# Windowed attention and a spatial-gating MLP on one core: batch 0's v in two long-run loads turned on chip, batch 0 in token halves, and a new order of the head

## Chip, cores and metric

One Trainium2 chip, one core. The metric is device microseconds from start to end of one execution, as the median of the runs shown. The engines are PE (matrix multiply), DVE (vector), ACT (scalar, activation functions), POOL (GpSimd) and SP (SyncE), on whose queue nearly all transfers are issued. Times called profile are from one profiled execution.

## What is computed

Eight batches of 8 heads, sequence 576, head width 64: causal attention over a window of 64 tokens, then a gated MLP whose gate mixes tokens.

```
scores = scale * np.matmul(q, k.transpose(0, 1, 3, 2))
mask = (rel >= 0) & (rel < window)              # rel = query - key, window = 64
attn = softmax(where(mask, scores, -1e9))
x = matmul(attn, v), heads side by side          # (8, 576, 512)
h = np.maximum(x @ w_in, 0.0)                    # (8, 576, 1024)
u, v = h[..., :512], h[..., 512:]
v_n = (v - mean(v)) / sqrt(var(v) + 1e-6)        # over the 512 features
v_s = np.einsum('ts,bsd->btd', w_spatial, v_n) + b_spatial[None, :, None]
out = (u * v_s) @ w_out                          # (8, 576, 512)
```

## The kernel before

The whole program is a list of steps, and its order is written out by hand. The string ORDER (from line 18) holds words such as `V0_2:PE:1`: step, engine, buffer or PSUM bank. Each engine executes its own steps in the order in which they stand there; between engines a step waits for the steps that it depends on and for its buffers. `PE` and `PH` are both the matmul engine (PH: a matmul of 128 output rows written as two of 64 that run side by side). `DQ` words are transfers on SP's queue, in the order written. There a transfer also waits until the one issued eight places before it has landed. PSUM is four single banks and two pairs.

The names, with batch b, head group g (four heads) and head pair u:

- **Loads.** `ldq`, `ldk` (L412) bring 128 x 1152 f32, 576 KB, in long runs: partition (head, 32 groups of 18 tokens). `ldv` (L433) brings v in token order instead, five transfers for each group: four of 128 tokens x 4 heads x 64 (128 KB, in runs of 256 bytes) and a last one of 64 tokens. `st` are the output stores (L656, L662).
- **Attention.** `cq`, `ck` cast q and k to f16 (ACT L292, DVE L300, POOL L295 in three parts); `tq`, `tk` are DVE's 32 x 32 stream transpose (L419). `cv` casts v to hv; `sl`, `su`, `s4` copy hv shifted by 64 partitions into hs. `S` scores (PE L479), `S_r` those of the last 64 tokens (L553); `E` exp (ACT L486, er L563); `M` the mask, a minimum (DVE L489, er L574); `Z` column sums (PE L502, L582), `N` and `n` their inverse by a logarithm and an exponential on ACT (L529, L531); `P` e times v (PE L514, edge P_r L597); `X` P times the inverse, x in f16 (DVE L522, edge X_r L606).
- **gMLP.** `V` and `U` are x times the two halves of w_in, by 128 tokens j or 128 features i (helper lines 614 and 617; the last 64 tokens of V at L702, fused with the batch before's O at L705). `Vr`, `Ur` are the relus on ACT (L669, L763), `Vb`, `Va` statistics (DVE L671, L673), `L1`, `L2` the inverse deviation (ACT L716, L718), `A` the normalisation to vn (DVE L728). `G` multiplies by the transposed w_spatial, `Ge` by u (DVE L797), `O` by w_out, `Oe` copies the result out of PSUM (ACT L647). `W`, `We` transpose w_spatial (PE L378) and copy it out; `cwin`, `cwsp`, `cwo` cast weights.
- **Fillers.** `D` are matmuls of a zero scratch tile (L862): 27 steps of two 512-column matmuls, two of them (D25, D26) of nine 128-column ones. Most stand in the head, D9 ahead of the first V, D17 ahead of G0.

Batch b+1's attention is threaded through batch b's gMLP. `V0_j` waits for all four `X0` (both head pairs of both groups), `U0_i` likewise, `O0_j` for all four `G0` tiles. `P3_r`, the edge P of batch 3, needs hs of v3, and so the copies `cv3_00` (POOL) and `su3_00` (ACT) behind the loads of v3.

Of the kernel before, what the change touches and what calls it, by code (L numbers as in the profile page):

```python
# [26 lines left out]
N0_01:ACT:2 cv0_00:ACT:1 N0_11:ACT:3 ldwin101:DQ su0_11:DVE M0_10:DVE D12:PE:0 Z0_10:PE:2 D20:PE:1
sl0_11:POOL tk1_0:DVE:4 sl0_00:ACT:1 N0_10:ACT:4 n0_11:ACT n0_10:ACT cq1_0:POOL:2 tq1_0:DVE:5
ldq1_1:DQ:2 ldk1_1:DQ:3 P0_10:PE:0 P0_11:PE:3 cwin110:ACT n0_01:ACT D11:PE:1 cv0_01:POOL
ldwin000:DQ:4 ldwin010:DQ:5 ldwin001:DQ ldwin011:DQ ldwsp1:DQ:6 X0_10:DVE:0 su0_00:DVE X0_11:DVE  # L30
n0_00:ACT sl0_01:POOL cb:POOL su0_01:POOL S1_0:PE:0:1 D25:PE:2 D13:PE:1 P0_00:PE:0 X0_00:DVE:1
E1_01:ACT:3 s40_1:ACT P0_01:PE:2 D9:PE:3 cwin111:POOL cwin100:POOL cwin101:POOL ck1_1:POOL:1
s40_0:ACT E1_00:ACT:2 cwin010:POOL X0_01:DVE cwin001:POOL cwin011:POOL V0_2:PE:1 M1_01:DVE
Vr0_2:ACT:0 n0_r:ACT P0_r:PE:3 Z1_01:PE:0 V0_0:PE:2 ldwsp3:DQ:0 M1_00:DVE N1_01:ACT:5 Vr0_0:ACT:1
cq1_1:DVE:3 Z1_00:PE:1 V0_3:PH:0 V0_1:PE:2 N1_00:ACT:4 cwin000:ACT Vr0_3:ACT:2 Vr0_1:ACT:3
ldwsp0:DQ:7 ldwsp4:DQ:1 ldwsp2:DQ:2 cwsp1:POOL:6 ldv1_00:DQ:2 ldq2_0:DQ:3 X0_r:DVE:0 tq1_1:DVE:7
Vb0_2:DVE:0 V0_4:PE:3 tk1_1:DVE:8 S1_1:PE:1:0 cwsp3:POOL:0 cwsp0:POOL:1 Vb0_0:DVE:1 Vb0_3:DVE:2
Vr0_4:ACT:4 Va0_3:DVE Vb0_4:DVE:3 Va0_4:DVE Va0_0:DVE Va0_2:DVE Vb0_1:DVE:4 Va0_1:DVE U0_2:PH:1
U0_3:PH:0 ldk2_0:DQ:4 U0_4:PE:2 ldv1_01:DQ ldv1_02:DQ ldv1_03:DQ E1_11:ACT:1 E1_10:ACT:0 cwsp2:POOL
cq2_0:POOL:0 M1_10:DVE ldv1_10:DQ:3 Ur0_2:ACT:0 L10:ACT:0 ldv1_11:DQ ldv1_12:DQ ldv1_13:DQ L20:ACT  # L40
ldv1_14:DQ ldq2_1:DQ:5 ldv1_04:DQ ldk2_1:DQ:6 ldwo00:DQ:0 ldwo01:DQ Ur0_4:ACT:1 S1_r:PE:0:1
Z1_10:PE:3 U0_0:PE:1 ldwo10:DQ:7 ldwo11:DQ U0_1:PE:2 E1_r0:ACT:0 Ur0_3:ACT:2 E1_r1:ACT Ur0_0:ACT:3
N1_10:ACT:3 A0_0:DVE:0 A0_3:DVE:1 cwsp4:DVE Ur0_1:ACT:4 W1:PE:0 W3:PE:1 W2:PE:3 W0:PE:2 A0_1:DVE:2
A0_4:DVE M1_11:DVE We1:DVE M1_r:DVE n1_00:ACT We2:ACT We3:ACT A0_2:DVE:3 We0:DVE W4:PE:0 ldq3_0:DQ:1
ldk3_0:DQ:2 ldv2_00:DQ:1 ck2_0:POOL:2 We4:DVE D17:PE:3 Z1_11:PE:1 Z1_r:PE:2 G0_0:PH:3 G0_1:PH:0
tq2_0:DVE:2 n1_10:ACT N1_11:ACT:0 tk2_0:DVE:3 Ge0_0:DVE:0 cv1_00:ACT:2 n1_01:ACT sl1_00:POOL:2
n1_11:ACT su1_00:ACT N1_r:ACT:2 cv1_01:POOL Ge0_1:DVE:1 su1_01:DVE G0_3:PH:1 sl1_01:POOL
cv1_10:ACT:3 Ge0_3:DVE:2 cv1_11:DVE S2_0:PE:0:1 P1_01:PE:2 P1_00:PE:3 X1_00:DVE:2 G0_2:PH:0
sl1_10:POOL:3 ldv2_01:DQ ldv2_02:DQ su1_10:ACT sl1_11:ACT E2_01:ACT:3 n1_r:ACT su1_11:POOL
s41_1:POOL P1_10:PE:1 X1_01:DVE P1_11:PE:3 G0_4:PE:2 X1_10:DVE:3 X1_11:DVE U1_1:PH:1 cq2_1:POOL:3  # L50
# [150 lines left out]
def kernel(  # L201
# [419 lines left out]
    def xr(b, r):  # L621
        return XB[b, r // 2].t[:, r % 2, :]
# [295 lines left out]
```

## Time and profile before

| what | us |
|---|---|
| median of three runs | 195.78 |
| the three runs | 195.34, 195.78, 196.4 |
| span of the profiled execution | 193.6 |
| the median less that span | 2.18 |
| PE busy, DVE busy, ACT busy, POOL busy | 184.9, 163.7, 157.1, 87.4 |

The span is the stretch that the profiler shows from first to last instruction; the execution's own time, measured outside, holds some 2 us more. A row of a timeline gives the start, the busy time, the engine, the line, the operation with its tiles and count, and in brackets how long the engine was idle before it and what released it. Matmul ends are modelled, so starts are the better measure on PE: the length of a row includes some time under the next one.

### The profile page before, as it was taken

The numbers are of one execution on the slowest core, as the hardware profiler recorded it, in microseconds if no ns is written. First come the engines' busy times: TensorE is split into PE (matmuls) and PEld (weight loads), VectorE is DVE, ScalarE is ACT, GpSimd is POOL, SyncE is SP. The second block draws the span as 40 slices with busy tenths as digits, with TensorE's granted clock in tenths as the row PEclk, the third lists the DMA queues.
The fourth block names the chain that finished last, engine by engine and source line by source line (L and its number), as shares of the span: only waits on it lengthen the run. The fifth ranks groups of instructions, "written<-read, shape, count | busy, mean of one in ns | idle before, by whom it ended". The sixth has DMA issues, their size and how long they took to land.

```text
span 193.6 us, 7606 instructions
## 1 busy us (share of the span) xinstructions
PE 184.9 (95%) x3218; PEld 107.0 (55%) x3218; DVE 163.7 (85%) x304; ACT 157.1 (81%) x282; POOL 87.4 (45%) x161
## 2 busy tenths in 40 slices
PE   7798998999999999999999999999999999999991
PEld 2352534556556664656665656565756565665560
DVE  4899899999999999998999999998996967468331
ACT  2269998998999999899979999999999875706430
POOL 4027775849932986701956577615641520000000
PEclk9999999999999999999999999999999999999999
DMA  5999999899989997619987999669958000600445
GB/s 177 373 316 290 391 355 333 168 275 373 242 205 332 261 335 179 149 38 289 367 230 184 310 310 282 196 177 218 306 125 266 22 3 0 224 30 0 135 166 191
DMA packets 50421, 42.73 MB, mean 221 GB/s; under 512 B 39377, under 2 KB 39761, under 8 KB 50386
## 3 DMA queue, kind: packets, MB, share of 16 engines
q1 hardware_dynamic: 50162, 42.04, 73.3%
q8 instruction: 25, 0.41, 0.9%
q10 hardware_dynamic: 224, 0.20, 0.3%
q14 instruction: 10, 0.08, 0.1%
HBM read 32.79 MB, written 9.44 MB: 218 GB/s over the span
## 4 chain that ended last, share of the span: by engine, by line
PE 70%; DVE 13%; ACT 9%; DMA 3%; issue 2%; SPq 1%
PE bank L617 50%; PE bank L614 4%; PE pair L479 4%; PE bank L514 3%; DMA nk<-in_k_dram 3%; PE bank L502 3%; ACT e L486 3%; DVE qT L419 2%; PE bank L702 2%; DVE e L489 2%; DVE kT L419 2%; DVE st L671 2%; DVE g L797 1%; DVE x L522 1%; ACT lz L529 1%
## 5 line engine op out<-in xcount | busy, mean ns | idle before, releaser
L617 PE MATMUL bank<-wspT,vn 128*64 128x512 f16 (+3 forms) x530 | 39.1, 296 | 0.0
L486 ACT ACTIVATE e<-pair 128x1024 f16<-128x1024 f32 x32 | 32.0, 1030 | 1.6 <-PE pair L479 1.4
L797 DVE TENSOR_TENSOR g<-bank,ru 128x512 f16<-128x512 f32 (+1 forms) x36 | 23.3, 654 | 9.4 <-PE bank L617 7.0
L647 ACT COPY ob<-bank 128x512 f32<-128x512 f32 (+1 forms) x38 | 21.9, 591 | 9.7 <-PE bank L617 8.4
L669 ACT ACTIVATE vs<-bank 128x512 f16<-128x512 f32 (+1 forms) x40 | 23.8, 602 | 7.1 <-PE bank L705 5.6
L617 PE MATMUL bank<-x,win 128*64 128x512 f16 (+2 forms) x304 | 29.1, 327 | 0.0
L617 PEld LDWEIGHTS <-vn 128*64 128x64 f16 (+1 forms) x530 | 20.8, 111 | 13.2 <-issue 0.2
L671 DVE BATCH_NORM_STATS2 st<-vs 128x6 f32<-128x512 f16 (+1 forms) x40 | 26.0, 670 | 2.3 <-ACT vs L669 2.2
L298 POOL COPY hs<-hv 64x512 f16<-64x512 f16 (+1 forms) x36 | 20.1, 585 | 16.3 <-ACT hv L292 8.4
L617 PE MATMUL bank<-win,x 128*64 128x512 f16 x216 | 27.0, 379 | 0.0
L617 PE MATMUL bank<-wout,g 128*64 128x512 f16 (+1 forms) x208 | 24.7, 371 | 0.0
L522 DVE TENSOR_TENSOR x<-bank,lz 128x512 f16<-128x512 f32 x32 | 21.2, 684 | 3.5 <-PE bank L514 2.2
L489 DVE TENSOR_TENSOR e<-e,mask 128x1024 f16<-128x1024 f16 x32 | 23.0, 725 | 0.5 <-ACT e L486 0.4
L763 ACT ACTIVATE ru<-bank 128x512 f32<-128x512 f32 (+1 forms) x38 | 21.6, 584 | 1.5 <-PE bank L617 0.8
L295 POOL CAST hk<-nk 128x384 f16<-128x384 f32 x36 | 19.4, 574 | 7.1 <-DMA nk<-in_k_dram 6.7
L529 ACT ACTIVATE lz<-bank 128x512 f32<-128x512 f32 x32 | 19.0, 599 | 1.9 <-PE bank L502 1.6
L298 POOL CAST hv<-nv 128x512 f16<-128x512 f32 x18 | 11.7, 661 | 18.8 <-DMA nv<-in_v_dram 18.7
L419 DVE STREAM_TRANSPOSE kT<-hk 128x576 f32<-128x576 f32 x16 | 19.9, 1241 | 0.2 <-ACT hk L292 0.2
L419 DVE STREAM_TRANSPOSE qT<-hq 128x576 f32<-128x576 f32 x16 | 19.8, 1237 | 0.2
L531 ACT ACTIVATE lz<-lz 128x512 f32<-128x512 f32 x32 | 19.6, 642 | 0.0
L295 POOL CAST hq<-nq 128x384 f16<-128x384 f32 x27 | 14.9, 588 | 10.3 <-DMA nq<-in_q_dram 7.8
L617 PEld LDWEIGHTS <-win 128*64 128x64 f16 x304 | 14.4, 110 | 9.2
(91 smaller groups left out, 298.9 us busy)
## 6 DMA issues: line engine op xcount, KB each, us to landing
nk<-in_k_dram SPq DMA_DIRECT2D x16, 576.0 KB, 6.6
nq<-in_q_dram SPq DMA_DIRECT2D x16, 576.0 KB, 6.1
nv<-in_v_dram SPq DMA_DIRECT2D x64, 128.0 KB, 5.9
out_dram<-ob SPq DMA_DIRECT2D x14, 512.0 KB, 5.8
wi<-in_moe_w_in_dram SPq DMA_DIRECT2D x8, 256.0 KB, 5.8
ws<-in_moe_w_spatial_dram SPq DMA_DIRECT2D x4, 288.0 KB, 7.6
nv<-in_v_dram SPq DMA_DIRECT2D x16, 64.0 KB, 4.5
wo<-in_moe_w_out_dram SPq DMA_DIRECT2D x4, 256.0 KB, 7.2
```

Of the source, the lines that this page charges most:

```text
L295: nc.gpsimd.tensor_copy(o[:, n:n + 384], i[:, n:n + 384])
L298: nc.gpsimd.tensor_copy(o[:, lo:hi, :, :], i[:, lo:hi, :, :])
L419: d = add(f"t{name}{b}_{g}", ("DVE", 1.09), key, lambda e: nc.vector.transpose(qt.t[:, :].rearrange("p (i j) -> p j i", j=18), h.t[:, :].b ...
L486: ex = add(f"E{b}_{g}{u}", ("ACT", 0.91), key, lambda e, u=u: nc.scalar.activation(e2[u].t[:, :, :], sc[u].t[:, :, :], AF.Exp, bias=0.0, s ...
L489: mins.append(add(f"M{b}_{g}{u}", ("DVE", 0.65), key, lambda e, u=u: nc.vector.tensor_tensor(e2[u].t[:, :, :], e2[u].t[:, :, :], mask[:, : ...
L522: lambda e, u=u, ob=ob, lz=lz: nc.vector.tensor_tensor(x.t[:, u, :], ob.t[:, :], lz.t[:, :], ALU.mult),
L617: nc.tensor.matmul(o[c:c + 64, :], w[:, c:c + 64], x, start=start, stop=stop)
L647: lambda e: (nc.vector.tensor_copy if last else nc.scalar.copy)(view(), m.t[rows, 0:n]),
L669: rl = add(f"Vr{b}_{j}", ("ACT", 0.49), key, lambda e: nc.scalar.activation(vs.t[0:jn, :], m.t[0:jn, :], AF.Relu), deps=[pv], acq=[vs], us ...
L671: s1 = add(f"Vb{b}_{j}", ("DVE", 0.6), key + 0.02, lambda e: nc.vector.bn_stats(st6.t[0:jn, 0:6], vs.t[0:jn, :]), deps=[rl], acq=[st6], us ...
L763: lambda e, m=m, ru=ru, n=n: nc.scalar.activation(ru.t[:, 0:n], m.t[:, 0:n], AF.Relu), deps=[pu], acq=[ru], uses=[m])))
L797: nc.vector.tensor_tensor(g.t[:, 0:n], m.t[:, 0:n], ru.t[:, 0:n], ALU.mult)
```

## The change

Six things, all but the last for batch 0 alone.

1. Its v is loaded like q and k (`ldvt0_0`, `ldvt0_1`, 128 x 1152), cast to f16 (`cvt`: group 0 on ACT, group 1 on POOL), turned in 32 x 32 blocks on DVE (`tvt`), then in 128 x 128 blocks on PE (`T0_g` eight, `T0_g4` two), and copied out of PSUM into hv by `cv0_00`, `cv0_01` (ACT) and `cv0_10`, `cv0_11` (DVE), every second element; `s40_g` copies out of PSUM on ACT. Ten small loads and two POOL casts of v go.
2. `Z0`, `P0`, `X0` work on both head pairs of one 256-token half instead of one head pair over 512 tokens. `V0_j` and `U0_i` then need the X of one half only; `U0`, `G0` and `O0` go by 256 tokens, with twice as many matmuls of 256 columns in U and G.
3. The relus and `Oe` may be put on DVE by the order; it puts them on ACT as before.
4. Fillers: 23 steps, all of two 512-column matmuls, D0 to D22, none behind the first V.
5. Casts move: `ck0_0`, `cq0_1` to ACT, `ck1_0`, `cq1_1` to POOL, and `ck0_1` to POOL.
6. ORDER is written anew. On PE the first part differs; from about G1_1 and V2_3 on it is the same sequence of steps. On SP the order differs further on.

The core of the diff:

```diff
+SPLIT = (0,)
+TURN = (0,)
+        if b in TURN:
+            vt, vd = one("vt", v, key + 0.002)
...
+                    for w in (0, 1):
+                        nc.tensor.transpose(o[0:sn, at + 128 * w:at + 128 * w + 128],
+                                            vT[:, 128 * c:128 * c + sn, w], id16[:, :])
...
+                        lambda e, lo=lo, hi=hi: cp(
+                            e, hv.t[:, lo:hi, :, :].rearrange("p c h (x w) -> p c w (h x)", w=2),
+                            m.t.bitcast(f16)[:, 256 * lo:256 * hi].rearrange(
+                                "p (c w x) -> p c w x", w=2, x=128)),
...
+                    for hh in range(4):
+                        w, p = hh % 2, hh // 2
+                        nc.tensor.matmul(zb.t[64 * w:64 * w + 64, 256 * p:256 * p + 256], ones[:, :],
+                                         e2[p].t[:, w, 256 * u:256 * u + 256], start=True, stop=True)
...
-                     deps=[XD[b, r] for r in range(4)] + [WIN[1, r] for r in range(4)],
+                     deps=[XD[b, r] for r in (range(4) if b not in SPLIT else (j // 2, 2 + j // 2))]
+                     + [WIN[1, r] for r in range(4)],
...
+                    if i < 4 and b in SPLIT:
+                        u = i // 2
+                        for f in (0, 1):
+                            c = 2 * (i % 2) + f
+                            for r in range(4):
+                                halves(f"U{b}_{i}", m.t[:, 256 * f:256 * f + 256],
+                                       w_in_sb[r][:, 128 * c:128 * c + 128],
+                                       xr(b, r)[:, 256 * u:256 * u + 256], r == 0, r == 3)
...
-            for c in range(2 if i < NWARM - NFILL else FILL):
-                n = 512 if i < NWARM - NFILL else 128
-                nc.tensor.matmul(m.t[:, 0:n], scratch[:, 0:128], scratch[:, 0:n], start=True, stop=True)
+            for c in range(2):
+                nc.tensor.matmul(m.t[:, :], scratch[:, 0:128], scratch[:, :], start=True, stop=True)
```

DVE up to batch 0's X, before (e2_0 are the masked scores, kT and qT the transposes for batch 1, hs the shifted copies of v, x0_0 and x0_1 batch 0's x of groups 0 and 1):

```order
L300 CAST hk1_0_285<-nk1_0_156 128x1152
L574 TENSOR_TENSOR er_0_275<-er_0_275,mask_88 128x512
L489 TENSOR_TENSOR e2_0_11_359<-e2_0_11_359,mask_88 128x1024
L300 COPY hs0_1_279<-hv0_1_154 64x512
L489 TENSOR_TENSOR e2_0_10_365<-e2_0_10_365,mask_88 128x1024
L419 STREAM_TRANSPOSE kT1_0_400<-hk1_0_285 128x18x32
L419 STREAM_TRANSPOSE qT1_0_412<-hq1_0_408 128x18x32
L522 TENSOR_TENSOR x0_1_461<-bank0_69,lz0_10_404 128x512
L300 COPY hs0_0_402<-hv0_0_385 64x512
L522 TENSOR_TENSOR x0_1_461<-bank3_72,lz0_11_387 128x512
L522 TENSOR_TENSOR x0_0_552<-bank0_69,lz0_00_357 128x512
L522 TENSOR_TENSOR x0_0_552<-bank2_71,lz0_01_383 128x512
```

The same place in the changed kernel (x0_4 is the x of the last 64 tokens):

```order
L302 COPY hv0_1_421<-bank3_72 128x2x2x128 x2
L539 TENSOR_TENSOR e2_0_11_389<-e2_0_11_389,mask_88 128x1024
L539 TENSOR_TENSOR e2_0_10_419<-e2_0_10_419,mask_88 128x1024
L302 COPY hs0_1_441<-hv0_1_421 64x512
L430 STREAM_TRANSPOSE kT1_0_455<-hk1_0_315 128x18x32
L302 COPY hs0_1_441<-hv0_1_421 64x512
L430 STREAM_TRANSPOSE qT1_0_487<-hq1_0_402 128x18x32
L576 TENSOR_TENSOR x0_0_517<-bank2_71,lz0_00_386 128x2x256
L727 TENSOR_TENSOR x0_4_580<-bank0_69,lz0_r_443 128x256
L576 TENSOR_TENSOR x0_1_600<-bank1_70,lz0_10_460 128x2x256
L576 TENSOR_TENSOR x0_0_517<-bank3_72,lz0_01_457 128x2x256
L576 TENSOR_TENSOR x0_1_600<-bank2_71,lz0_11_489 128x2x256
```

The cast of k1_0 has left DVE, the two evictions of turned v (x2 in the first row) have come, and the x of the last 64 tokens stands second among the X, where before it stood behind batch 1's masks. The order by token halves lets the first two V steps do with the first three X rows.

SP's queue around the loads of v3, before (nv3_0 is v of batch 3, group 0; ob are output tiles):

```order
L662 DMA out_0_dram<-ob0_0_1547 128x2x512
L433 DMA nv3_0_1936<-in_v_dram 128x4x64
L433 DMA nv3_1_1466<-in_v_dram 64x4x64
L433 DMA nv3_0_1936<-in_v_dram 128x4x64 x3
L433 DMA nv4_0_2045<-in_v_dram 128x4x64 x2
L433 DMA nv3_0_1936<-in_v_dram 64x4x64
L656 DMA out_0_dram<-ob1_4_1977 64x512
```

And in the changed kernel:

```order
L783 DMA out_0_dram<-ob0_2_1443 128x2x512
L777 DMA out_0_dram<-ob1_4_2061 64x512
L488 DMA nv4_0_1395<-in_v_dram 128x4x64
L783 DMA out_0_dram<-ob0_0_1650 128x2x512
L488 DMA nv3_0_2112<-in_v_dram 128x4x64 x2
L488 DMA nv3_0_2112<-in_v_dram 64x4x64
L488 DMA nv3_0_2112<-in_v_dram 128x4x64
L488 DMA nv3_1_1299<-in_v_dram 64x4x64
L488 DMA nv3_0_2112<-in_v_dram 128x4x64
```

The store of batch 1's last 64 tokens (`st1_4`, ob1_4) stood behind the loads of v3 and now stands ahead of all six of them.

406 lines of the change are left out of this document (260 added, 146 removed).

## The prediction

> **What bounds the kernel now.** I read the page's busy shares first, then the busy time of each engine by stretch, then the timeline of the matmul engine (PE) around its gaps, and last the timelines of the engine or queue that each gap names.
>
> ```profile
> span 193.6 us, 7606 instructions
> PE 184.9 (95%) x3218; PEld 107.0 (55%) x3218; DVE 163.7 (85%) x304; ACT 157.1 (81%) x282; POOL 87.4 (45%) x161
> ```
>
> The shares say PE; where it has room only the stretches tell (columns: start:end, length, busy PE, PEld, DVE, ACT, POOL with counts, granted clock, DMA share, GB/s).
>
> ```profile
> 10.00:20.00 10.00, 9.25 (x145) 4.15 (x143) 9.80 (x14) 8.34 (x14) 5.38 (x8) 1.00 1.13 307
> ...
> 24.00:30.00 6.00, 5.56 (x47) 2.14 (x51) 5.57 (x8) 5.49 (x10) 4.56 (x7) 1.00 1.08 339
> ...
> 46.00:80.00 34.00, 33.95 (x584) 19.51 (x580) 33.03 (x60) 32.59 (x62) 23.35 (x42) 1.00 0.92 264
> 80.00:90.00 10.00, 9.67 (x250) 6.36 (x247) 9.48 (x18) 9.31 (x15) 2.10 (x4) 1.00 0.47 106
> 90.00:186.00 96.00, 96.00 (x1677) 57.66 (x1674) 79.41 (x152) 77.89 (x142) 35.58 (x67) 1.00 0.63 184
> ```
>
> From 46 to 186 us PE is idle for 0.05 + 0.33 us; so a microsecond won before 46 reaches the end unless something else holds PE later. In the head the busy PE is mostly filler (L862); what bounds there is DVE, 9.80 of 10 us. So three places matter: when the first real gMLP matmul starts, what PE loses or wastes between it and batch 1's first U, and the one later gap, near 86.6. PE's rows there (start, length, what ended the idle time):
>
> ```profile
> 9.26 0.67 PE L479 MATMUL pair<-qT,kT 32*128 32x128 f16 x56 [1.12 <-DVE qT L419]
> ...
> 23.42 0.39 PE L614 MATMUL bank<-win,x 128*128 128x512 f16 x1
> 24.02 0.82 PE L614 MATMUL bank<-win,x 128*128 128x512 f16 x3 [0.21 <-DVE x L522]
> 24.77 0.32 PE L597 MATMUL bank<-er,hs 128*64 128x64 f16 x8
> 24.92 0.39 PE L502 MATMUL bank<-e,ones 128*64 128x512 f16 x2
> ...
> 28.37 1.05 PE L702 MATMUL bank<-win,x 128*64 128x512 f16 x4
> 29.85 0.67 PE L479 MATMUL pair<-qT,kT 32*128 32x128 f16 x56 [0.42 <-DVE kT L419]
> ...
> 32.30 0.64 PE L614 MATMUL bank<-x,win 128*128 128x64 f16 x16
> ...
> 33.41 0.41 PE L502 MATMUL bank<-e,ones 128*64 128x512 f16 x2 [0.24 <-DVE e L489]
> ...
> 37.80 0.61 PE L862 MATMUL bank<-scratch 128*128 128x512 f16 x2
> 38.34 0.41 PE L502 MATMUL bank<-e,ones 128*64 128x512 f16 x2
> ...
> 45.53 1.05 PE L617 MATMUL bank<-x,win 128*64 128x512 f16 x8
> ```
>
> V of batch 0 starts at 23.42, halts for an X, waits 0.42 for batch 1's k transpose and 0.24 for a masked e; one filler (D17) stands in the stream at 37.80; batch 1's U starts at 45.53.
>
> **The change part by part.** *A, up to the first V.* Loads and the chain to the first S (SyncE's queue, DVE, ACT):
>
> ```profile
> 1.21 0.38 SPq L412 DMA_DIRECT2D nk<-in_k_dram  x1
> ...
> 2.10 0.43 SPq L412 DMA_DIRECT2D nk<-in_k_dram  x1
> ...
> 5.26 0.76 DVE L300 CAST hk<-nk 128x1152 f16<-128x1152 f32 x1 [1.66 <-DMA nk<-in_k_dram]
> 8.20 1.15 ACT L292 CAST hk<-nk 128x1152 f16<-128x1152 f32 x1 [6.11 <-DMA nk<-in_k_dram]
> 10.00 1.94 ACT L486 ACTIVATE e<-pair 128x1024 f16<-128x1024 f32 x2 [0.65 <-PE pair L479]
> 9.38 1.26 DVE L419 STREAM_TRANSPOSE kT<-hk 128x576 f32<-128x576 f32 x1 [0.18 <-ACT hk L292]
> ...
> 13.83 0.69 DVE L489 TENSOR_TENSOR e<-e,mask 128x1024 f16<-128x1024 f16 x1
> ...
> 22.67 1.29 DVE L522 TENSOR_TENSOR x<-bank,lz 128x512 f16<-128x512 f32 x2 [0.18 <-PE bank L514]
> ```
>
> The first k lands 4.05 us after its issue, and the second k, two big loads on, 2.94 later: 1.47 each. The changed queue starts with q, k, v, k, q, v, k, q; with the first issue 0.4 earlier they land at about 4.9, 6.3, 7.8, 9.3, 10.7, 12.2, 13.7 and 15.1. The second load is cast on ACT (1.15) to 7.5 and transposed (1.26) to 8.8, which starts the first S, against 9.26. E starts 0.74 after S (10.00 − 9.26) and takes about 1.0, so the first mask starts near 10.55. From there I take DVE as unbroken: four masks and the edge mask at 0.65, five transposes at 1.15 (back to back they come at less than the row's 1.26), four hs copies at up to 0.29, two evictions of turned v, then X0_00 0.65 and X0_r 0.4, behind which V0_4 can start; X0_10 is done inside V0_4's four matmuls.
>
> The evictions have no row in before. The nearest is DVE copying 128 x 576 f16 out of a bank with a plain destination (here with the hs copies, from the groups that keep shapes apart); the other bound is the 0.69 of the mask above:
>
> ```profile
> L300 DVE COPY hs<-hv 64x512 f16<-64x512 f16 x4 | 1.2, 294 | 0.1
> L300 DVE COPY wspT<-bank 128x576 f16<-128x576 f16 x2 | 0.9, 450 | 0.1
> ```
>
> That is 0.40 for 512 columns, to 0.69; the new copy writes every second element, so I take 0.55. [...]
>
> Sum: 3.25 + 5.75 + 1.1 + 1.1 + 1.05 = 12.25, so V0_4 at 22.8 if DVE never waits; it waited 0.18 + 0.31 + 0.18 in before's head, and I allow 0.2: 23.0. **A is −0.4** (−0.9 with quick evictions and short masks, +0.9 with slow Pool casts, below). Masks come one for one as before; DVE loses four casts (0.76 each) and gains two transposes and two evictions (3.4), so its work is about equal: the gain is order, and X0_01, which held the first V, is now behind it. The PE transposes of v (20 short matmuls) take the place of fillers. Splitting Z, P, U, G by 256 columns adds matmuls but no columns; the 16-matmul row at 32.30 shows 64-column matmuls each with its own weight load at 0.04 us, so loads do not limit 256-column ones: 0 us.
>
> *B, from the first V to U of batch 1.* Starts less work give the stalls: 23.42 to 24.02 is 0.60 for one matmul of some 0.22 (1.05 for four against 0.82 for three), 0.38 lost; the wait of S at 29.85 is 0.42, that at 33.41 is 0.24; D17 is 38.34 − 37.80 = 0.54; P0_r (24.77 to 24.92, 0.15) moves ahead of V. Sum 1.73. All go: V0_4 goes first, S1_1 stands behind more gMLP work, D17 is dropped. What is late next: G0 comes earlier and needs A, cast weights and their transposes, and S1_r and Z1_01 now stand among U: I charge 0.3 (0 to 0.7, an estimate from the stalls they replace, 0.24 and 0.42). **B is −1.45.** The new cover is thin: DVE was 5.57 of 6 busy there.
>
> *C, the gap near 86.6.* Batch 3's edge P stands behind hs of v3:
>
> ```profile
> 67.06 10.66 SPq L433 DMA_DIRECT2D nv<-in_v_dram  x8
> ...
> 74.88 0.58 ACT L647 COPY ob<-bank 64x512 f32<-64x512 f32 x1
> ...
> 78.57 0.61 POOL L298 CAST hv<-nv 128x512 f16<-128x512 f32 x1 [0.33 <-DMA nv<-in_v_dram]
> ...
> 85.43 1.04 ACT L292 COPY hs<-hv 64x1024 f16<-64x1024 f16 x1
> 86.62 0.32 PE L597 MATMUL bank<-er,hs 128*64 128x64 f16 x8 [0.33 <-DVE e L489]
> ```
>
> The page's list of transfers (count, KB, median us from issue to landing) has the two kinds that matter:
>
> ```profile
> nv<-in_v_dram SPq DMA_DIRECT2D x64, 128.0 KB, 5.9
> ...
> out_dram<-ob SPq DMA_DIRECT2D x8, 128.0 KB, 3.4
> ```
>
> In before the v3 loads went ahead of the store st1_4, whose data is ready at 75.46. In the changed queue this store stands ahead of them: all six v loads queue behind a wait on ACT, and the last, six rows later on a queue where each transfer also waits for the one eight rows back, follows close on the store's landing. With A and B won the store goes at 73.5 and lands 3.4 later; the last v load issues at about 77 and lands 3.4 to 5.9 later, 80.4 to 82.9; cast 0.61 and hs copy 1.04 give 82.1 to 84.6, against 86.47 − 1.9 = 84.6 needed. **C is 0, to +0.3.** Elsewhere the order of PE's work is the same from V2 on, and its 96.00 of 96 us carries the gain to the end; the tail has the same steps.
>
> Sum: −0.4 − 1.45 + 0 = −1.9 on the 193.6 us span, 191.7. The three runs' median is 195.78 (195.34 to 196.4), 2.2 more than the span; I take this as fixed: **193.9 us**.
>
> **The rivals.** *Pool casts set the head.* The change gives Pool the casts of k0_1, v0_1, k1_0 and q1_0 in a row, then three hs copies and four w_in casts that every V needs. Pool's three-part casts cost 1.41 in a quiet stretch, and far more where loads and DVE are busy:
>
> ```profile
> 21.69 1.72 POOL L300 CAST win<-wi 128x512 f16<-128x512 f32 x3
> 25.20 2.28 POOL L295 CAST hk<-nk 128x384 f16<-128x384 f32 x3 [1.79 <-DMA nk<-in_k_dram]
> ...
> 34.13 2.69 POOL L295 CAST hq<-nq 128x384 f16<-128x384 f32 x3 [1.39 <-DMA nq<-in_q_dram]
> ...
> 75.53 1.41 POOL L295 CAST hq<-nq 128x384 f16<-128x384 f32 x3
> ```
>
> The first starts when k0_1 lands, at 9.3, the second not before 12.2. At 1.41 the four end at 16.5; three hs copies (some 0.55 each, as the weight casts) and four weight casts, 2.3, bring it to 20.5; at 2.28 it is 19.1 and 23.1, just in time; at 2.69: 12.0, 14.9, 17.6, 20.3, then 4.0 of copies and weights, 24.3. V0_4 then starts 1.3 late, and −1.9 becomes −0.6: **195.2**. Against it: the head's casts would meet a Pool with half its time free (5.38 of 10). [...]
>
> *A larger gain.* Quick evictions, no waits of DVE, no new stalls in B: −0.9 − 1.7 = −2.6, **193.2**. For it: the stream after V is otherwise the same work. Against: DVE has no slack to hide anything.
>
> *The slow side: the store ahead of the v3 loads.* If they issue at the rate of the row at 67.06 (10.66 over 8, 1.33 each) from 74.5, the sixth goes at 82.5; landing 4.7 later (middle of 3.4 and 5.9), cast and copy bring hs to 88.8 against 86.47 in before. PE stands still at P3_r, all of A and B is lost and 2.3 more: **198.1**. It decides once v3's last load lands after 84.8. For it: DMA busy 0.92 from 46 to 80, and this gap already exists. Against: those 10.66 us held waits of the queue that need not recur, and from 80 DMA share is 0.47.
>
> *The change does nothing for the time*: the head wins, but DVE and ACT (33.03 and 32.59 of 34 us from 46 to 80) turn out to set batches 1 and 2, and both only move work about: **195.8**.
>
> **How the numbers follow.** A measurement of this kernel can tell about 0.5% from no change, 0.98 us: faster is below 194.8, slower above 196.8. Chances: forecast (193.3 to 194.8) 0.5; larger gain (below 193.3) 0.13; Pool casts or saturated DVE and ACT (194.8 to 196.8) 0.22; slow side 0.15. So faster 0.63, same 0.22, slower 0.15. The range runs from 192.7 (just past the larger gain, its lowest part, some 0.04, left out) to 196.9 (the slow side left out). The forecast's own range is 193.3 to 194.8.
>
> **What would show it.** Right: V0_4 near 23.0 with no hole behind it, batch 1's first U near 43.6, P3_r near 84.7, span near 191.7. Wrong in A: idle DVE ahead of a transpose, released by Pool; V0_4 waiting for a win cast on Pool. Wrong in B: new PE waits for A, Ge or hs of batch 1 between 25 and 45. Wrong in C: P3_r's idle time over 1 us, with v3 loads issued after 79. If U1 gains 2 us and P3_r starts where it did, C has eaten it.

## The result, and the profile after

The changed kernel is slower: a median of 203.22 us (200.95 to 203.97, four runs) against 196.09 (195.34 to 197.63) for the kernel before in the same comparison, a ratio of 1.031 [1.023, 1.039]. The forecast was 193.9 with 192.7 to 196.9 around it; even the rival on the slow side, at 198.1, was too low. The profiled execution is the longest of the four (203.97, span 202.3, mean clock 0.975); a second trace, of the same kernel run again with the experiments (median 202.25, span 199.1), is used beside it. Ratios here and below are of undisturbed runs alone, medians of all, so the two need not divide out.

The page after, span, busy shares and the clock in 40 slices:

```profile
span 202.3 us, 7762 instructions
PE 188.8 (93%) x3290; PEld 113.8 (56%) x3290; DVE 165.1 (82%) x302; ACT 159.3 (79%) x283; POOL 95.6 (47%) x177
...
PEclk9999759999999999999999999999879999999999
```

There are 72 more matmuls and 72 more weight loads than before (3290 against 3218), and the clock, which was full in every stretch quoted of before, has two dents (the second trace has the first of them alone). By stretch (columns as in the prediction):

```profile
10.00:20.00 10.00, 7.87 (x187) 4.54 (x185) 8.35 (x12) 8.38 (x12) 6.31 (x14) 1.00 1.01 371
20.00:24.00 4.00, 2.74 (x47) 1.76 (x46) 3.87 (x6) 3.62 (x7) 3.89 (x6) 0.84 1.04 401
24.00:30.00 6.00, 5.25 (x92) 2.74 (x87) 5.77 (x8) 3.47 (x7) 5.94 (x12) 0.54 0.48 140
...
46.00:80.00 34.00, 32.96 (x669) 19.65 (x666) 33.21 (x55) 31.65 (x57) 25.31 (x45) 1.00 0.81 232
...
140.00:150.00 10.00, 7.65 (x192) 4.91 (x188) 7.13 (x12) 6.22 (x12) 5.46 (x10) 0.83 0.76 205
```

From 10 to 20 us PE is busy 7.87 of 10 where it was 9.25; from 24 to 30 the clock is about half; and PE loses 2.35 us of ten from 140 on, where before nothing was lost. PE's rows at those places:

```profile
10.43 0.67 PE L529 MATMUL pair<-qT,kT 32*128 32x128 f16 x56
...
25.05 1.04 PE L600 MATMUL pair<-qT,kT 32*128 32x128 f16 x56 [0.76 <-DVE qT L430]
...
26.46 1.89 PE L824 MATMUL bank<-win,x 128*64 128x512 f16 x4
28.29 4.02 PE L735 MATMUL bank<-win,x 128*128 128x512 f16 x15
...
32.36 1.91 PE L735 MATMUL bank<-x,win 128*128 128x256 f16 x16
...
48.40 1.05 PE L738 MATMUL bank<-x,win 128*64 128x512 f16 x8
...
69.33 0.22 PE L635 MATMUL bank<-e,hs 128*64 128x64 f16 x2 [0.57 <-issue]
...
91.09 0.32 PE L718 MATMUL bank<-er,hs 128*64 128x64 f16 x8 [0.34 <-ACT hs L294]
...
143.37 0.25 PE L635 MATMUL bank<-e,hv 128*64 128x128 f16 x2
...
146.24 0.26 PE L635 MATMUL bank<-e,hv 128*64 128x64 f16 x2 [2.35 <-issue]
...
148.64 1.22 PE L738 MATMUL bank<-wout,g 128*64 128x512 f16 x8
```

The same stretch of batch 6's P in before, first and last row:

```profile
138.61 0.25 PE L514 MATMUL bank<-e,hv 128*64 128x128 f16 x2
...
140.23 1.03 PE L617 MATMUL bank<-wout,g 128*64 128x512 f16 x8
```

From these starts the 8.7 us between the two spans (202.3 − 193.6) can be laid out, and beside them the 5.5 us of the second trace (its starts are 25.95, 47.72, 141.97 and 145.91):

| stretch of PE's work | before | after | difference | difference, second trace |
|---|---|---|---|---|
| start to the first V | 23.42 | 26.46 | +3.04 | +2.53 |
| first V to batch 1's first U (45.53, 48.40) | 22.11 | 21.94 | −0.17 | −0.34 |
| that U to batch 6's P (138.61, 143.37) | 93.08 | 94.97 | +1.89 | +1.17 |
| batch 6's P to the O behind it (140.23, 148.64) | 1.62 | 5.27 | +3.65 | +2.32 |
| that O to the end of the span | 53.37 | 53.66 | +0.29 | −0.18 |

The sums are 8.70 and 5.50; the medians differ by 7.1. Two things stand out that the prediction does not contain: "issue" waits, in which PE waits for nothing that the trace names, and a PE at half clock.

### The profile page after: what moved, and what is told of

Read it like the earlier page. It is cut to its first block, busy times and chain, and to the rows that moved or that the text cites. A ratio compares the mean times of both kernels' runs of the same rounds, so it can differ in the third digit from the quotient of the medians.

```text
span 202.3 us, 7762 instructions
## 1 busy us (share of the span) xinstructions
PE 188.8 (93%) x3290; PEld 113.8 (56%) x3290; DVE 165.1 (82%) x302; ACT 159.3 (79%) x283; POOL 95.6 (47%) x177
## 4 chain that ended last, share of the span: by engine, by line
PE 65%; ACT 12%; DVE 9%; DMA 5%; issue 5%; SPq 3%; ACTq 0%
PE bank L738 45%; PE bank L1006 5%; PE bank L824 3%; PE pair L600 3%; DMA nv<-in_v_dram 3%; ACT e L607 3%; PE bank L635 3%; PE bank L735 2%; SPq L488 2%; PE bank L623 2%; DMA out_dram<-ob 2%; ACT ob L294 2%; ACT lz L650 2%; DVE vn L850 1%; ACT ru L306 1%
## 5 line engine op out<-in xcount | busy, mean ns | idle before, releaser
L738 PE MATMUL bank<-wspT,vn 128*64 128x512 f16 (+5 forms) x550 | 38.5, 287 | 0.5 <-DVE vn L850 0.3
L300 POOL COPY hs<-hv 64x512 f16<-64x512 f16 (+1 forms) x40 | 23.5, 614 | 13.8 <-ACT hv L294 12.9
L738 PE MATMUL bank<-x,win 128*64 128x512 f16 (+3 forms) x312 | 29.3, 323 | 0.0
L607 ACT ACTIVATE e<-pair 128x1024 f16<-128x1024 f32 x28 | 28.0, 1032 | 0.9 <-PE pair L600 0.6
L738 PE MATMUL bank<-wout,g 128*64 128x512 f16 (+1 forms) x232 | 27.8, 374 | 0.0
L297 POOL CAST hk<-nk 128x384 f16<-128x384 f32 x42 | 22.1, 564 | 10.3 <-DMA nk<-in_k_dram 9.0
L300 POOL CAST hv<-nv 128x512 f16<-128x512 f32 x20 | 13.7, 697 | 26.1 <-DMA nv<-in_v_dram 26.0
L643 DVE TENSOR_TENSOR x<-bank,lz 128x512 f16<-128x512 f32 x28 | 18.7, 684 | 5.7 <-PE bank L635 3.7
L610 DVE TENSOR_TENSOR e<-e,mask 128x1024 f16<-128x1024 f16 x28 | 21.6, 777 | 0.0
L738 PEld LDWEIGHTS <-g 128*64 128x64 f16 x232 | 13.2, 111 | 10.3 <-issue 0.7
```

The costliest lines, as they stand in the source:

```text
L297: nc.gpsimd.tensor_copy(o[:, n:n + 384], i[:, n:n + 384])
L300: nc.gpsimd.tensor_copy(o[:, lo:hi, :, :], i[:, lo:hi, :, :])
L607: ex = add(f"E{b}_{g}{u}", ("ACT", 0.91), key, lambda e, u=u: nc.scalar.activation(e2[u].t[:, :, :], sc[u].t[:, :, :], AF.Exp, bias=0.0, s ...
L610: mins.append(add(f"M{b}_{g}{u}", ("DVE", 0.65), key, lambda e, u=u: nc.vector.tensor_tensor(e2[u].t[:, :, :], e2[u].t[:, :, :], mask[:, : ...
L738: nc.tensor.matmul(o[c:c + 64, :], w[:, c:c + 64], x, start=start, stop=stop)
```

## The experiments

### The same kernel again, and the head's queue and gaps

> The changed kernel once more, unedited, beside the runs of the kernel before on the same chip, for a second trace. If the half clock of PE at 22.9 to 29.3 us and the 2.35 us hold of PE at 143.9 us come from the order itself, both are here again, with batch 1's first U near 48.4 and a time of 201 to 204. If they are accidents of one execution, at least one is missing and the time is nearer to 200.

Measured: 202.25 us (200.85 to 202.7), 1.030 [1.026, 1.035]. First V at 25.95; clock 0.63 from 20 to 24 us and 0.68 from 24 to 30; one issue wait after the head, 2.14 us, at 144.62 and at the same matmul as the 2.35 above. So the late first V, the low clock in the head and the hold at batch 6's P are the kernel's own, not one run's. The second dent of the clock is not: here it is 1.00 behind the hold, and the stretch around the hold costs 2.32, not 3.65.

Two edits of the head followed, each alone and then both. One puts fillers into the gaps between 18 and 25 us, on the score pairs, which are free there:

```diff
+D23:PE:1 D24:PE:1        behind T0_14
+D22:PE:0 D25:PE:1        behind Z0_r
-D22:PE:3                 from ahead of Z0_10
+D26:PE:0                 behind Z0_11
+D27:PE:1 D28:PE:0        behind P0_10
```

> Seven fillers (two 512-column matmuls each) are put into PE's gaps between 18.6 and 25 us of the changed kernel; they write to banks of the score pairs that stand empty there. Clock theory (PE is too little busy there, the clock halves, S1_0 and the first V steps run at half speed): granted clock 1.00 throughout the head, S1_0 0.6 instead of 1.04, four V matmuls in 0.9 instead of 1.9, batch 1's first U about 2 us earlier (46.4), time 2 us lower. Queue theory (what is lost is that 32 filler matmuls stand ahead of the first S): no change, 203. DVE theory (the vector chain ahead of X is simply longer): the clock is mended, but V0_4 starts no earlier than 26, gain of about 1.5.

The other lets batch 0's first S pass four of the fillers:

```diff
+S0_0:PE:0:1              ahead of D12
 D12 D13 D14 D15
-S0_0:PE:0:1
```

> Four of the sixteen fillers ahead of the first S (D12 to D15) are moved behind it. Queue theory: S0_0 starts at 8.7 instead of 10.43, the first mask at 10.5 instead of 12.2, all of the head 1.7 us earlier, batch 1's first U near 46.7, time 1.7 lower. Clock theory alone: S0_0 earlier, but the gaps between 17 and 25 stay or grow and the clock halves as before; gain of 0 to 1.7. DVE theory: k0_1 and v0_1 (landing at 9.8 and 12.6) hold DVE next, so less than 1 us is won.

> Both edits: four fillers behind the first S, seven in the gaps. If queue and clock are the two causes in the head, batch 1's first U is at 44.5 to 45.0, against 45.53 in the kernel before and 48.4 in the changed one, and the time is 3.5 to 4 lower than the changed kernel, 199 to 199.5; what is then left above 196 is lost later (from 48 to 150 us). If the later losses come from the late head as well, the time falls below 197.

Measured: fillers 201.93, 1.026 [1.020, 1.033]; earlier S 200.61, 1.025 [1.018, 1.031]; both 201.68, 1.030 [1.024, 1.036]. Alone, neither moves the first V much: it starts at 26.52 with the fillers, where the clock is whole but the first S starts at 10.88, and at 26.07 with the earlier S (9.38), where the clock from 24 to 30 us is 0.72. With both, the first S starts at 8.59 instead of 10.43 (9.61 in the second trace), the clock is whole, and the first V starts at 24.55 instead of 26.46. The stretches with both edits:

```profile
20.00:24.00 4.00, 3.69 (x85) 2.05 (x88) 3.90 (x5) 3.79 (x8) 3.94 (x8) 1.00 1.04 403
24.00:30.00 6.00, 6.00 (x93) 3.35 (x77) 6.00 (x10) 5.50 (x10) 5.87 (x10) 1.00 0.57 161
```

Yet the time is not better. The waits of PE in the same trace (released by, total us, times, longest) show where the gain went:

```profile
PE bank L630 <- issue: 2.3, 2, 1.5
...
PE bank L733 <- issue: 1.3, 1, 1.3
...
PE pair L669 <- issue: 0.2, 1, 0.2
```

That is 3.8 us of issue waits, against 2.14 in the unchanged kernel's second trace. The net six filler steps are 24 instructions more, but they are not needed for a new wait: the earlier S alone, with none more, has one of 0.72 at 49.94 beside the hold of 2.10. What an issue wait is had to be settled first.

### What the issue waits are

Count PE's instructions in the order of the trace, each matmul and its weight load as one each. The 2.35 us wait stands ahead of instruction 5052, that at 69.33 ahead of 2238: 19 x 256 + 188 and 8 x 256 + 190. In every trace of this study with such a wait after the head it stands at 186 to 190 beyond a multiple of 256, at places such as 1470, 2238, 4028, 5052. The page's list of queues has one for instructions:

```profile
q8 instruction: 25, 0.41, 0.9%
```

25 transfers, 0.41 MB: 16 KB each, and 3290 matmuls with their weight loads are 25.7 times 256 instructions; before has 25 as well, and its 3218 are 25.1 times. So the count fits one transfer for every 256 of PE's instructions; that these transfers are PE's is my inference from it. The theory, then: PE's program comes in blocks of 256, PE runs out of fetched instructions in dense stretches that lie across a boundary between two blocks, at a cost of up to 2.35 us, and the 144 instructions that the change adds moved the boundaries. The rival: the holds come from something else in the new order, and the 256 is chance.

The kernel before, its order unchanged, with 144 more PE instructions of the same columns: twelve fillers of two 512-column matmuls as eight of 128 (CUT holds D0 to D4, D6 to D8 and D10 to D13).

```diff
-for c in range(2 if i < NWARM - NFILL else FILL):
-    n = 512 if i < NWARM - NFILL else 128
+for c in range(8 if i in CUT else 2 if i < NWARM - NFILL else FILL):
+    n = 512 if i < NWARM - NFILL and i not in CUT else 128
```

> The kernel before, with 12 of its fillers written as eight 128-column matmuls instead of two of 512: the same PE time and place, 144 more PE instructions, as many as the changed kernel has more. Fetch theory (PE halts where its program crosses into a block of 256 instructions that has not yet been fetched; in the five traces of the changed order every hold put down to issue lies at instruction 188 to 190 modulo 256): a hold of 1.5 to 2.3 us appears at PE instruction 5052, near 141 us, perhaps others at 1470, 2238 and 5564, and the time rises by 2 to 4 us to 198 to 200 with nothing else changed. Rival (the holds come from the late head or from the transfers' new order): no hold, 196.

Measured: 200.67 (198.02 to 202.52), 1.013 [1.007, 1.020]; the ratio rests on two runs, 198.02 and 199.33. Its waits and its row at batch 6's P:

```profile
PE bank L514 <- issue: 1.9, 2, 1.0
```

```profile
140.22 0.19 PE L514 MATMUL bank<-e,hs 128*64 128x64 f16 x1
141.41 0.19 PE L514 MATMUL bank<-e,hs 128*64 128x64 f16 x1 [0.99 <-issue]
```

The two waits stand at 2238 and 5050, the places of the changed kernel, in an order that has none of its edits. The last matmul ends 2.5 us later than in before; the two waits are 1.9 of that, and the first V, 0.33 later, is half of the rest. So the new order is not needed for these waits; the number of instructions ahead is enough.

The other direction: the changed kernel, and the version with both head edits, with so many cut fillers that the difference from before becomes 252, almost a whole block (nine fillers, +108, and with both edits seven, D0 to D6, +84).

```diff
-for c in range(2):
+n = 128 if i in (0, 1, 2, 3, 4, 5, 6, 7, 8) else 512
+for c in range(1024 // n):
```

> The changed kernel with nine of its first fillers written as eight 128-column matmuls: 108 more PE instructions, 252 more than before in all, no step moved. Fetch theory: the hold of 2.1 to 2.3 us at PE instruction 5052 is gone, the half clock in the head stays, time 200 to 200.5 instead of 202.5 to 203. Rival: no change.

> The kernel with four fillers behind the first S and seven in the gaps, and in addition seven fillers written as eight 128-column matmuls: 84 more PE instructions at the same PE time, so that the program after the head lies against the blocks of 256 instructions as in the kernel before (252 more in all). Fetch theory: the holds put down to issue (1.3, 0.7 and 1.5 us with fillers alone) are gone, batch 1's first U stays near 45, the last matmul comes 3.5 us earlier (191), time 197.5 to 198. Rival (transfers' order or late loads): holds stay, 201.

Measured: the changed kernel 200.21, 1.020 [1.015, 1.025], against 1.030 [1.026, 1.035] before the cut: the intervals do not meet (that of the first comparison, [1.023, 1.039], meets it at the edge). With both head edits 198.44 (ten runs), 1.010 [1.007, 1.013], against 1.030 [1.024, 1.036]. The waits at batch 6's P are gone in both; one of 0.88 and 0.92 us remains at instruction 1470. Two things follow: the boundaries cost the changed kernel about 2 us (1.0%), and once they are moved the two head edits, which seemed worthless, are worth another 1.0%.

The theory is not the whole, though. The kernel before with 252 more instructions, the edit of the 144 with 21 fillers cut:

```diff
+CUT = range(21)
```

> The kernel before with 21 fillers written as eight 128-column matmuls: 252 more PE instructions, so that blocks of 256 lie as in before save for 4. Fetch theory: no hold put down to issue, 195.8, the same as before, although more instructions were added than in the kernel with 144 (198 to 202). Rival (more and smaller matmuls in the head cost by themselves): slower, by more than the 1.3 per cent of the kernel with 144.

Measured: 197.37, 1.008 [1.005, 1.011], with no issue wait behind the head but one in it:

```profile
15.77 0.33 PE L479 MATMUL pair<-qT,kT 32*128 32x64 f16 x20 [0.93 <-issue]
```

Its first V is at 24.58, 1.16 later than before. So a whole block more does give back the places, and a wait of 0.93 us stands in the head instead. How long a wait is also differs from trace to trace of like kernels (2.35 and 2.14; 0.57 and none at 2238), so the place alone does not set it. The instruction transfer at the 2.35 us hold starts when the hold does, at 143.8, and takes 0.95; PE goes on 1.5 us after it has ended, and nothing in the trace tells why. The DMA engines are full there (share 1.14 from 144 to 146). That the loads slow the fetch is possible from this, and not shown.

### The split alone

The kernel before with only the token halves of batch 0 (Z, P, X, U, G, O), its loads of v and its order, but V0_0 and V0_2 changing places with their statistics; fillers cut so that the places of the boundaries stay (260 instructions more, a block and four). Its sum of one head pair stands ahead of the mask that it now needs, so one sum takes unmasked scores and waits for one mask less.

```diff
+SPLIT = (0,)
+TURN = ()
 order: V0_2 <-> V0_0, Vr0_2 <-> Vr0_0, Vb0_2 <-> Vb0_0, Va0_2 <-> Va0_0
```

> Batch 0 by token halves alone: the order and the loads of v of the kernel before, V0_0 exchanged with V0_2 so that the first V needs only the first half's X, and 12 fillers cut so that the instruction blocks lie as in before (260 more). Theory that the halves are sound and the head's order, loads and fillers lost the time: the first V no longer halts for X0_01 (0.38 us), 0.2 to 0.5 us faster than before, 195.6. Theory that halves cost by themselves (twice the matmuls of 256 columns): 0.5 us or more slower, 196.6 or above.

Measured: 198.26, 1.010 [1.006, 1.013]. With the sum behind its mask:

```diff
-Z0_11:PE:3 N0_11:ACT:3   from behind D4
+Z0_11:PE:3 N0_11:ACT:3   behind M0_10
```

> Batch 0 by token halves alone, with the order and loads of before, V0_0 first, instruction blocks as in before; the sum Z0_11 (and its logarithm N0_11) now stand behind the mask of head pair 0, which they need. Halves sound by themselves: first V at 23.8 or earlier, no hold behind it, 195.5 to 196. Halves cost by themselves (both masks ahead of every sum, twice the U and G matmuls): the head waits for masks three times (0.2 to 0.7 us each), first V near 24, last matmul about 1 us later than in before, 196.8 to 197.5.

Measured: 199.19, 1.011 [1.007, 1.016]; first V at 25.03, against 23.42. Every sum of a half now needs the masks of both head pairs. PE's rows that wait for them:

```profile
15.03 0.30 PE L548 MATMUL bank<-e,ones 128*64 128x256 f16 x2 [0.72 <-DVE e L534]
...
19.23 0.41 PE L548 MATMUL bank<-e,ones 128*64 128x256 f16 x4 [1.31 <-DVE e L534]
```

Against the kernel before the split by halves is 1% slower in an order made for whole head pairs, and its sums wait for masks. That the split itself costs this is not shown: the kernel before with 252 more instructions and no split was 1.008 [1.005, 1.011], and the trace of the version just shown also has an issue wait of 1.15 at instruction 1470 (46.37 us). With the count held, no difference is clear.

### The store ahead of the v3 loads

SP's rows in the changed kernel:

```profile
67.13 1.07 SPq L783 DMA_DIRECT2D out_dram<-ob  x1
79.64 0.51 SPq L777 DMA_DIRECT2D out_dram<-ob  x1
```

The queue stands from 68.2 to 79.64 for the data of st1_4, as the prediction said that it might. The place that suffers is another. With both head edits and the cut fillers, PE and then ACT:

```profile
84.42 0.25 PE L630 MATMUL bank<-e,hv 128*64 128x128 f16 x2 [1.56 <-ACT ob L289]
```

```profile
83.79 0.59 ACT L289 COPY ob<-bank 128x512 f32<-128x512 f32 x1 [2.03 <-DMA out_dram<-ob]
```

P3_11 waits 1.56 for its PSUM bank, the bank for Oe1_2, and Oe1_2 for its output buffer, which st0_0, behind st1_4 in the queue, had not yet emptied. In the changed kernel with cut fillers the same wait is 0.50; in its own profile everything is 3 us later and the wait does not show. One word moved:

```diff
-st1_4:DQ                 behind Ur2_1
+st1_4:DQ                 behind ldv4_01 (behind the v3 loads, as before)
```

> The aligned kernel with early first S and filled gaps (198.4), and one word moved on SP: the store of batch 1's last 64 tokens stands behind the six loads of v3 again and so no longer ahead of the store of batch 0's first two blocks. Theory (the store waits for ACT from 68 to 77 us with all of SP's queue behind it; the output buffer of batch 0's first store comes free late, ACT's copy waits 2.0 us for it and PE 1.56 us at 84.4 for the bank): the hold of 1.56 us at P3_11 is gone, batch 3's edge P starts near 88.5 to 89 instead of 90.5, time 197 or a little below. Rival (those waits move elsewhere, to hs of v3): P3_r still waits, 198.4.

Measured: 196.91, 1.006 [1.003, 1.009], against 1.010 [1.007, 1.013]. The times only lean that way, but the trace is plain; the same P3_11, and then P3_r, with no idle time:

```profile
81.25 0.22 PE L630 MATMUL bank<-e,hv 128*64 128x128 f16 x2
...
87.03 0.32 PE L713 MATMUL bank<-er,hs 128*64 128x64 f16 x8
```

Three more cut fillers (D7 to D9, 36 instructions) then moved the boundaries once more:

> The same with three more fillers written as eight 128-column matmuls, 36 more PE instructions (288 more than before): by the block times of the traces this moves the block boundary from within batch 2's first S to ahead of it, where a block lasts about 1 us longer. Fetch theory: the hold of 0.9 us at PE instruction 1470 (46 us) shrinks or goes and none appears elsewhere, time 0.5 to 1 below that of the kernel without it, 196.0 to 196.5, about the kernel before. Rival: the hold stays at 1470, no change.

Measured: 196.6 (twelve runs), 1.0035 [1.0015, 1.0055]. This is the change with its mishaps mended; it is still not faster than before.

### What is left: DVE in the head, and term B by itself

DVE's rows in that last version, from the first mask to the last x that V0_4 needs:

```profile
10.68 0.69 DVE L534 TENSOR_TENSOR e<-e,mask 128x1024 f16<-128x1024 f16 x1
11.77 1.26 DVE L425 STREAM_TRANSPOSE kT<-hk 128x576 f32<-128x576 f32 x1 [0.40 <-POOL hk L292]
...
16.28 0.36 DVE L297 COPY hs<-hv 64x512 f16<-64x512 f16 x1
...
17.20 1.34 DVE L297 COPY hv<-bank 128x512 f16<-128x512 f16 x2
18.44 0.67 DVE L534 TENSOR_TENSOR e<-e,mask 128x1024 f16<-128x1024 f16 x1
19.03 1.10 DVE L534 TENSOR_TENSOR e<-e,mask 128x1024 f16<-128x1024 f16 x1
20.16 0.59 DVE L297 COPY hs<-hv 64x512 f16<-64x512 f16 x1
...
24.27 0.40 DVE L722 TENSOR_TENSOR x<-bank,lz_r 128x256 f16<-128x256 f32 x1
```

Of the two masks at 18.44 and 19.03 the first takes 0.67, like the 0.69 at 10.68, and the second 1.10; the hs copy takes 0.59 where 0.29 was the mean before. POOL copies hs in three parts from 18.16 on (2.44 us), the two of 64 x 512 in 0.98 each. To see whether POOL does that, two POOL copies of 64 x 512 f16 were put behind POOL's cast of v, beside an early mask (they write a tile that is overwritten later):

```diff
+Q0:POOL Q1:POOL          behind cvt0_1
+nc.gpsimd.tensor_copy(wspT[0][0:64, 0:512], scratch[0:64, :])
```

> The realigned kernel (store back) with two more copies of 64 x 512 on POOL, right behind its cast of v0_1, where POOL stands idle while DVE masks and transposes; what they write is overwritten later. Contention theory for term A (DVE's masks of 0.85 instead of 0.6 us and its hs copies of 0.59 and 0.46 instead of 0.29 come from copies on POOL at the same time): the mask M0_01 at 14.4, which took 0.69 with POOL idle, takes 0.8 to 0.9, and POOL's copies take longer than 0.61. Rival (they are slow for another reason): 0.69 as before.

Measured, one run: 197.79. DVE's rows, an hs part and a mask beside the copies (POOL, 13.84 to 15.1), and the next hs copy:

```profile
14.22 0.30 DVE L297 COPY hs<-hv 64x256 f16<-64x256 f16 x1
14.89 0.76 DVE L534 TENSOR_TENSOR e<-e,mask 128x1024 f16<-128x1024 f16 x1 [0.37 <-ACT e L531]
...
16.85 0.67 DVE L297 COPY hs<-hv 64x512 f16<-64x512 f16 x1
```

The hs part went from 0.22 to 0.30, the mask from 0.69 to 0.76, short of the 0.8 to 0.9 expected; a fifth of a microsecond of it lies beside a copy, the rest beside a POOL cast. POOL's own two copies, expected to take longer than 0.61, took 0.61 each. And the hs copy went from 0.36 to 0.67 with a POOL cast beside it in both versions. So DVE is slower in places where POOL works beside it, but that the copies are the cause is not shown; what makes DVE slow there stays open.

Term B was tried in the kernel before, in two steps, with the number of instructions kept (D24 as four 256-column matmuls):

```diff
-D17:PE:3
```

> The kernel before without the filler D17 that stands ahead of G0 (one filler written as four 256-column matmuls, so that the count of PE instructions stays). The term of the prediction for D17 is 0.54 us: 195.4 if every microsecond won before 46 us reaches the end (last matmul at 189.0 instead of 189.5). Rival (the next wait takes it back, or DVE and ACT set the pace): 195.9, no change.

```diff
-S1_1                     behind tk1_1
+S1_1                     behind U0_2
-Z1_10                    ahead of U0_0
+Z1_10                    behind U0_0
```

> The kernel before without D17 and with two steps of PE moved: S1_1 behind U0_2, Z1_10 behind U0_0, so that the waits of 0.42 (k transpose of batch 1) and 0.24 us (its masked scores) meet other work. These are three of the five parts of term B, worth 0.54 + 0.42 + 0.24 = 1.2 us, with the head, the loads and the instruction blocks as in before. If B was right and what failed is elsewhere: 194.7, faster than both kernels. If B's gains are taken by new waits (masks and sums of batch 1 come 0.5 us later): 195.4 to 195.9.

Measured: without D17 195.81, 0.998 [0.996, 1.001]; with the moves as well 197.02, 1.005 [1.002, 1.008]. The filler's 0.54 us would be a ratio of 0.9972: the interval holds that and no change. From the first V to batch 1's first U the three traces take 22.11 (before), 22.24 and 22.31: nothing is won there. PE's rows without D17:

```profile
33.58 0.41 PE L497 MATMUL bank<-e,ones 128*64 128x512 f16 x2 [0.61 <-DVE e L484]
38.37 0.41 PE L497 MATMUL bank<-e,ones 128*64 128x512 f16 x2 [0.32 <-ACT wspT L287]
```

and with the moves:

```profile
33.55 0.30 PE L548 MATMUL pair<-qT,kT 32*128 32x64 f16 x14 [0.38 <-ACT e L481]
34.04 1.02 PE L609 MATMUL bank<-x,win 128*128 128x512 f16 x4 [0.19 <-ACT ru L758]
```

The 0.32 stands where D17 stood, the 0.38 and 0.19 near the moved steps; the 0.61 lies ahead of D17's place and comes from a mask that took 1.03 in this execution instead of 0.66. So in the old order each stall that goes is followed by a wait for the next thing that ACT or DVE has to finish. The 1.005 with the moves is not all theirs, though: in its trace the first V, ahead of both moves, is 0.60 later than in before, and an issue wait of 0.79 stands at 106.77, at instruction 3516, 188 beyond a multiple of 256, although the number of instructions is that of before.

## Why the prediction was wrong, step by step

**The steps that failed.** There are two of about equal weight. The first is a term put at nothing: "Splitting Z, P, U, G by 256 columns adds matmuls but no columns [...]: 0 us." I priced the weight loads and not the number of instructions. In the version with the split alone 144 of the 260 instructions are the split's (the cut fillers bring 116); in the changed kernel the transposes of v and the dropped fillers nearly cancel beside it. 144 more instructions, with nothing else changed, cost the kernel before 1.3% [0.7, 2.0], some 2.6 us; putting the boundaries back gave the changed kernel 1.0%, some 2.0. The second is A: the head came late for reasons that the sum for A does not hold, and the two edits of the head gave another 1.0%.

The loss can be followed down a ladder of versions: changed 1.030; boundaries moved 1.020; head edits too 1.010; store back 1.006; boundaries moved again 1.0035. The first two steps lie outside each other's intervals; the last two do not, and rest on the traces.

**A, −0.4 to the first V: wrong, +3.0 in the profile, +2.5 in the second trace.** The loads landed as worked out, and kT was ready at 8.56, 0.24 ahead of my 8.8. But the first S started at 10.43 (9.61 in the second trace): the 32 filler matmuls of D0 to D15 stand ahead of it in PE's queue and end then. I took DVE as the bound of the head and never counted PE's own queue. Two rows of DVE in the changed kernel, the transpose and the first mask (forecast 10.55):

```profile
7.30 1.26 DVE L430 STREAM_TRANSPOSE kT<-hk 128x576 f32<-128x576 f32 x1 [0.51 <-ACT hk L294]
...
12.22 0.69 DVE L539 TENSOR_TENSOR e<-e,mask 128x1024 f16<-128x1024 f16 x1 [1.53 <-ACT e L536]
```

With the S moved up, the mask is at 10.68 and the rest of A's sum can be read term by term, from start to start in DVE's rows of the mended version: masks 3.55 (forecast 3.25), transposes 6.05 (5.75), hs copies 1.75 (1.1), evictions 1.24 (1.1), the two X 1.0 (1.05), idle 0.40 (0.2). That is 13.99 against 12.45, and V0_4 at 24.74 instead of 23.0: **A is +1.3 even when nothing goes wrong ahead of it** (+1.1 to +1.4 in four traces with both head edits). The hs copies are the largest miss: I took 0.29 from rows of before, and here they come at 0.25 to 0.62. The evictions came at 0.62 to 0.67 (the row of two at 17.20 takes 1.34), nearer to 0.69, the slow one of my two bounds, than to the 0.55 that I took.

On top of this came the clock. In the changed kernel PE works in short pieces from 16 to 25 us with gaps of 0.2 to 0.9, and the S at 25.05 takes 1.04 for what is 0.67 at full clock, V0_4 1.89 for 1.03. From 20 to 24 and from 24 to 30 us the clock is 1.00 in the three traces with fillers in the gaps that I read there (fillers alone, both edits, the mended version); without them it was 0.84 and 0.54 (the changed kernel), 0.63 and 0.68 (again), 0.85 and 0.53 (with its boundaries moved), 1.00 and 0.72 (earlier S alone). I wrote that PE's transposes "take the place of fillers"; they did not fill the time.

**B, −1.45 from the first V to batch 1's U: right in the mended version, lost in the changed one.** PE's rows of the version with the store back and the boundaries moved:

```profile
24.74 1.03 PE L819 MATMUL bank<-win,x 128*64 128x512 f16 x4
25.71 3.63 PE L730 MATMUL bank<-win,x 128*128 128x512 f16 x16
29.17 1.91 PE L730 MATMUL bank<-x,win 128*128 128x256 f16 x16
...
45.26 1.05 PE L733 MATMUL bank<-x,win 128*64 128x512 f16 x8
```

That is 20.52 us against 22.11 in before: −1.6 (the terms of the forecast give −1.43, written −1.45), for the same steps of PE but for D17 and P0_r. In the changed kernel it was −0.2: V0_4 took 1.83 from its start to that of the next V where it takes 0.97 at full clock, and the V behind it 4.07 (28.29 to 32.36) instead of 3.46. So the part of the change that was to pay does pay, and A's +1.3 takes nearly all of it: U of batch 1 starts 0.27 earlier than before. Behind it the mended version's profile loses that again: 0.43 in a wait of G1 for vn at 61.50, which before does not have and the changed kernel has too (0.34 at 64.67), and 0.49 in an issue wait at 110.99.

**C, 0 to +0.3, and the slow rival.** The rival's cause was there, a queue that stands for a store, and its victim was not. I followed the v3 loads to P3_r, which waited 0.34, as before (0.58 in the second trace). I did not follow the stores behind that store to the output buffers, the banks and P3_11: 0.50 to 1.56 where the head is quick enough to show it.

**The other rivals.** Pool's casts did not set the changed kernel's head: the four came at 1.40, 1.56, 1.40 and 1.51, near the quiet 1.41. In the mended version, where DVE gets there sooner, the first takes 1.93 and holds a transpose for 0.40: a small part of this rival is there. The larger gain and the change that does nothing were not it either. "Its 96.00 of 96 us carries the gain to the end" was wrong as well: that stretch holds the dense P of batch 6, where the issue wait of 2.35 us fell. Of the 1.89 us between batch 1's U and there, idle time explains about 1.1, the wait at 69.33 half of that; the rest I have not followed.

## What to carry to other kernels

Count instructions as well as columns: where PE is fed without a gap, an edit far ahead that changes their number can move an issue wait into a dense stretch (here 144 more, and two waits of 1.9 us in all), so compare two orders only with the count held, or with several counts. Where a stretch waits for one engine, read the other engines' queues ahead of it too: a filler delays the real work that stands behind it in its queue, and yet here fillers kept the clock whole where the real work came in pieces (1.00 from 24 to 30 us, against 0.54 in the changed kernel). When a transfer that waits goes ahead on a queue, follow every transfer behind it, stores and their buffers too, not only the load that one has in mind.

## What the hardware showed that I had not expected

- PE stands for 0.2 to 2.35 us at places a multiple of 256 instructions apart, to within four. With 25 transfers of 16 KB on the instruction queue, about one for every 256 instructions, that points to instruction fetch, which no run shows by itself. Before had no such wait in its profile.
- The clock fell to about half (0.54 from 24 to 30 us) without a long idle time: the longest gap of PE between 16 and 25 us is 0.90 us (1.16 in the second trace, where the clock was 0.68). Here 7.87 us of work in the 10 up to 20 us and 2.74 in the 4 behind them, much of it short matmuls, did not hold it.
- After the 2.35 us hold the clock was 0.50 from 146 to 148 us, and the stretch cost 3.65 us more than before; after the 2.14 us hold of the second trace it stayed at 1.00, and the stretch cost 2.32. A hold of this length can be followed by half clock, and need not be.
- While POOL copied hs (0.98 a copy, against 0.61 in the run with two copies more), one of DVE's two masks took 1.10 instead of 0.69 and an hs copy 0.59 instead of 0.29 to 0.36.
